# Attention beside an MLP on one core: output products in halves ahead of the values products, and a reordered VectorE queue

## The chip, the cores and the metric

One Trainium2 chip, one core of it. The metric is the time of one execution in microseconds (us) on the device. Engines: PE (TensorE: matmuls; PEld its weight loads), DVE (VectorE), ACT (ScalarE), POOL (GpSimd), SP (SyncE, which here only issues DMAs). All operands are float32; some matmuls use the float32r type, for which the kernel splits values into a high part and a low rest.

## What is computed

With x of 2048 tokens by 448 channels:

```python
g = sigmoid((x * gate_w).sum(-1, keepdims=True))
q = heads(x @ wq)            # 16 heads of 28
k = x @ wk; v = x @ wv       # one head, shared by all queries
p = softmax(q @ k.T * 28 ** -0.5)
a = (p @ v).merge_heads() @ wo
h = gelu(layernorm(x) @ w1)  # its four quarters shifted by 1, -1, 2, -2 tokens
x1 = x + shifted(h) @ w2
b = x1 + gelu(layernorm(x1) @ w3) @ w4
out = g * a + (1 - g) * b
```

## The kernel before, in words

The program has three stages on one core, and its order is the order in which the Python code issues it (manual_schedule): each engine takes its own instructions strictly in that order and waits by semaphores for the others.

1. Projections of queries, keys and values, and the shifted mixing with w1 and w2 (up to L647).
2. The MLP with w3 and w4 (L649 to L740), in four blocks of 512 tokens. The very last of its 14 column blocks isn't finished there: its gelu result is kept (gf_late, L667), and its product with w4 is done in stage 3 as a filler. At the stage's end DVE adds the accumulated products to x1 (L738).
3. Attention (L743 to the end). The 16 heads are taken in groups of four, the tokens in blocks of 512. A **unit** u is one block with one group, so there are 16 units (NU), block after block with four groups each. The 2048 keys of a unit come in 16 tiles of 128 (NT), two per pass of the loop at L862. One pass is called a **cycle** here; a unit has eight, i = 0 to 7, and c counts them from 0 to 128 over all units (the last one only finishes).

A cycle does, in this order of issue:

- score tile A (scores, L197 to L203): for four heads, three rounds of four matmuls that work beside each other on 32 rows each. Two heads land in single PSUM banks (s0, s1), two in a pair of banks (pairs[0]).
- ACT takes the exponential of s0 and of s1 (exps, L843); DVE moves the pair to SBUF (L870).
- score tile B in the same way, into s2, s3_ and pairs[1]; ACT takes the exponentials of s2, s3_, pairs[1], and last, in place, of A's moved pair.
- the values products (values, L854) of the previous cycle's two tiles, 16 matmul rows in the trace, into bank s0; DVE adds them to the unit's running sum (values_end, L784 and L786).
- extra work by i: at i = 0 the finished sums of the previous unit leave by DMA (L791); at i = 1 DVE takes their reciprocal (recip, L794) and two DMAs spread it over the partitions; at i = 3 DVE normalises the previous unit (norm, L807), and the maximum for the next unit's scores is prepared (max_part L210 and L212 in bank s1, then max_end with eight small DMAs); at i = 4 to 7 one output product each (wo_job, L817): four column-tiled matmuls of 448 columns (by_columns, L812; eight matmul rows in the trace) into s1, and one DVE instruction (L828) that weights them with the gate and adds them up; at i = 6 the queries of a later unit are split (q_begin, L194 and L195) and the next ones fetched. In unit 0 the four products of gf_late with w4 (w4_job, L834) stand in place of the output products.

The four single banks change places each cycle: what is s0, s1 in one cycle is s2, s3_ in the next (L865). So score tile B of a cycle writes the banks that the values products and the output product of the cycle before have used, and must wait until DVE has read them. The two pairs don't change.

The last unit's normalisation and output are done in a tail (from L906) that the change touches only in the names of banks and helpers.

Of the kernel before, what the change touches and what calls it, by code (L numbers as in the profile page):

```python
# [9 lines left out]
F32 = mybir.dt.float32  # L10
F32R = mybir.dt.float32r
AF = mybir.ActivationFunctionType
ALU = mybir.AluOpType
# [3 lines left out]
P = 128  # L17
# [24 lines left out]
def gated_mix_kernel(  # L42
# [206 lines left out]
    with tc.tile_pool(name="s1b", bufs=1) as s1b, \  # L249
# [263 lines left out]
        high_w2(0)  # L513
        high_w2(1)

        def first(m):
# [8 lines left out]
        stage_w1(0, first)  # L525

        def second(m):
            if m < 2:
# [120 lines left out]
    with tc.tile_pool(name="s2", bufs=1, reuse_waits="tile") as s2, \  # L649
# [36 lines left out]
        for b in range(NB):  # L686
            acc = [ps2.tile([P, 512], F32, tag="acc", bufs=4, name=f"acc_{b}_{t}") for t in range(4)]
            gs = {}
            for f in range(NF):
                if f == 9 and b + 1 < NB:  # L690
                    mv, rs = layernorm_stats(s2a, b + 1)
                if f == 10 and b + 1 < NB:
                    xt4 = big(f"xt4_{b + 1}")[:, 0:4 * D].rearrange("p (f t j) -> p f t j", f=NE, t=4)
                if f in (10, 11) and b + 1 < NB:
                    for t in (2 * f - 20, 2 * f - 19):
                        xn = s2a.tile([P, 512], F32, tag="xn", bufs=1, name=f"xn_{b + 1}_{t}")[:, 0:D]
                        layernorm_norm(b + 1, t, mv, rs, xn, xt4)
# [36 lines left out]
            for t in range(4):  # L734
                if b < NB - 1:
                    w4_part(NF - 1, t, gs[NF - 1], acc)
                xt = x1[:, 4 * b + t, :]
                nc.vector.tensor_add(xt, xt, acc[t][:, 0:D])  # L738
        assert not fills
    ctx2.close()  # L740


    with tc.tile_pool(name="s3", bufs=1, reuse_waits="tile") as s3, \  # L743
# [16 lines left out]
        def q_fetch(u):  # L760
            if u < NU:
                q_load(u, qr)
# [46 lines left out]
        def by_columns(ps, a, t, w):  # L809
            for i in range(4):  # L810
                c = t * P + 32 * i
                nc.tensor.matmul(ps[32 * i:32 * i + 32, :], a[:, c:c + 32], w, start=True, stop=True,  # L812
                                 tile_position=(0, 32 * i))

        ot_of = {}

        def wo_job(u, t, bank, end=None):  # L817
            b, g = divmod(u, NG)
            n = 4 * b + t
            ps = bank[:, 0:D]  # L820
            by_columns(ps, on_of[u], t, wof[:, g, :])
            before = x1[:, n, :] if g == 0 else ot_of[n]
            if g == 0:
                ot_of[n] = s3.tile([P, D], F32, tag="ot", bufs=5, name=f"ot_{n}")
            if end:
                end(t, n, ps, before)
                return
            nc.vector.scalar_tensor_tensor(ot_of[n], ps, gg[:, n:n + 1], before, op0=ALU.mult, op1=ALU.add)  # L828
            if g == NG - 1:
                nc.sync.dma_start(out[0, n * P:(n + 1) * P, :], ot_of[n])  # L830

        weigh_x1(NT - 4, NT)

        def w4_job(t, bank):  # L834
            n = NT - 4 + t
            ps = bank[:, 0:D]
            by_columns(ps, gf_late, t, w4_late)
            nc.vector.scalar_tensor_tensor(x1[:, n, :], ps, gi[:, n:n + 1], x1[:, n, :], op0=ALU.mult, op1=ALU.add)

        p_of = {}  # L840

# [12 lines left out]
                nc.tensor.matmul(pv[32 * j:32 * j + 32, :], vext[:, kt, :], p[:, j],  # L854
                                 start=first, stop=last, tile_position=(0, 32 * j))
# [3 lines left out]
        sums, norms = [], []  # L859
        pv = None  # L860

        for c in range(NU * NT // 2 + 1):  # L862
            u, i = divmod(c, NT // 2)
            k = 2 * c
            s0, s1, s2, s3_ = singles if c % 2 == 0 else singles[2:] + singles[:2]  # L865
            if u < NU:
                pa = score_tiles(u, 2 * i, s0, s1, pairs[0])
                exps(pa, left, s0.unsqueeze(1))
                exps(pa, right, s1.unsqueeze(1))
                nc.vector.tensor_copy(pa[:, both], pairs[0])  # L870
                pb = score_tiles(u, 2 * i + 1, s2, s3_, pairs[1])
                exps(pb, left, s2.unsqueeze(1))
                exps(pb, right, s3_.unsqueeze(1))
                exps(pb, both, pairs[1])
                exps(pa, both)
            if c:
                v = divmod(c - 1, NT // 2)[0]
                pv = s0
                values(k - 2, pv, True, False)
                values(k - 1, pv, False, True)  # L880
                if (v, i) != (NU - 1, 0):
                    values_end(v, pv)
                if i == 0 and v < NU - 1:
                    sums.append(sums_begin(v))
            if u == NU:
                break
            if i == 1 and sums:
                norms.append(recip(*sums.pop()))
            if i == 3 and norms:
                w = norms[0][0]  # L890
                norm(*norms.pop())
                jobs += [lambda bank, w=w, t=t: wo_job(w, t, bank) for t in range(4)]
            if i == 3 and u + 1 < NU:
                max_part(u + 1, range(4), s1)
                max_end(u + 1)
            elif i > 3 and jobs:
                jobs.pop(0)(s1)
            if i == 1 and u == 0:
                q_begin(1)
                q_fetch(2)  # L900
            if i == 6 and u + 2 < NU:
                q_begin(u + 2)
                q_fetch(u + 3)
        assert not sums and not norms and not jobs

        u = NU - 1  # L906
        part = o_of.pop(u)
# [4 lines left out]
        b0, b1, b2, b3 = singles  # L912
# [25 lines left out]
        def end(t, n, ps, before):  # L938
            if t == 1:
                nc.scalar.activation(y, ps, AF.Copy, scale=gg[:, n:n + 1])  # L940
                nc.gpsimd.tensor_tensor(ot_of[n], y, before, ALU.add)
            else:
                nc.vector.scalar_tensor_tensor(ot_of[n], ps, gg[:, n:n + 1], before, op0=ALU.mult, op1=ALU.add)
            queue = nc.scalar if t == 1 else nc.sync
            queue.dma_start(out[0, n * P:(n + 1) * P, :], ot_of[n])

        def tail_wo(t):
            wo_job(u, t, wo_banks[t], end)

        def keep_warm(n):  # L950
            for _ in range(n):
# [40 lines left out]
        with tc.If(again > 0, label="redo"):  # L992
            for b in range(NB):
                for g in range(NG):
# [15 lines left out]
                    banks.append(pv)  # L1010
                    norm(*recip(*sums_begin(u), False))
                    for t in range(4):
                        wo_job(u, t, bank(f"wo2_{u}_{t}"))


_OUTS = [((1, S, D), "float32")]
# [48 lines left out]
```

## Time and profile before

| | us |
|---|---|
| median of 3 runs | 963.37 (962.07 to 963.64) |
| the profiled execution | 963.59 |
| its span, first to last instruction | 961.7 |

How to read the rows: a group of instructions is given as line, engine, operation, what it writes and reads, shape and count, then busy time in us and mean ns of one, then how long the engine was idle just before them and who ended that. A row of the timeline is the start in us, the length in us, engine, line, operation, operands, count of merged instructions, and in brackets the idle time before and who ended it. Matmuls are pipelined, so their rows overlap, and a row's length is not the pace: the distance between starts is.

### The profile page before, as it was taken

How to read it: one execution, taken by the hardware profiler on the slowest of the kernel's cores; microseconds unless marked ns; L12 is line 12 of the kernel's file. 1: busy time of each engine (PE TensorE's matmuls, PEld its weight loads, DVE VectorE, ACT ScalarE, POOL GpSimd, SP SyncE). 2: the span in 40 equal slices, each digit the busy share in tenths (PEclk: the TensorE clock that was granted, in tenths of full speed). 3: DMA queues.
4: the chain of work that ended last, by engine and by line, in shares of the span. 5: the costliest groups of instructions: out<-in, count | busy, mean ns of one | idle time of the engine just before them, and what ended most of it. 6: DMA issues, size and time to landing. Idle time of an engine off the chain costs nothing.

```text
span 961.7 us, 18356 instructions
## 1 busy us (share of the span) xinstructions
PE 943.5 (98%) x7575; PEld 562.6 (59%) x7575; DVE 497.2 (52%) x766; ACT 634.2 (66%) x1005; POOL 80.9 (8%) x111
## 2 busy tenths in 40 slices
PE   9999999999999999999999999999999999999996
PEld 7788888888888888644343443344434444433432
DVE  4663454523423411265565565666566566655653
ACT  5532454322222221499989989989998998999893
POOL 3342500100003400200000000000000000000000
PEclk9999999999999999999999999999999999999999
DMA  9823452300300300100000010000010000110001
GB/s 319 274 75 92 117 175 72 102 1 1 82 2 1 82 1 1 48 12 24 14 21 14 23 50 13 23 12 23 23 52 11 14 23 12 43 32 6 9 14 42
DMA packets 40419, 46.99 MB, mean 49 GB/s; under 512 B 10120, under 2 KB 28488, under 8 KB 40328
## 3 DMA queue, kind: packets, MB, share of 16 engines
q1 hardware_dynamic: 37304, 40.27, 13.8%
q10 hardware_dynamic: 3024, 5.47, 1.6%
q8 instruction: 61, 1.00, 0.4%
q14 instruction: 30, 0.25, 0.1%
HBM read 32.56 MB, written 11.67 MB: 46 GB/s over the span
## 4 chain that ended last, share of the span: by engine, by line
PE 76%; ACT 18%; DVE 3%; issue 2%; DVEq 0%
ACT p L843 18%; PE bank L854 16%; PE bank L203 12%; PE bank L812 5%; PE acc L682 5%; PE acc L684 5%; PE acc L683 5%; PE g L135 4%; PE g L136 4%; PE g L137 4%; PE hs L460 1%; PE pair L203 1%; PE hs L461 1%; PE g L138 1%; PE g L139 1%
## 5 line engine op out<-in xcount | busy, mean ns | idle before, releaser
L843 ACT ACTIVATE p<-bank 128x512 f32<-128x512 f32 x512 | 269.9, 638 | 44.5 <-PE pair L203 37.7
L854 PE MATMUL bank<-p,vext 128*32 128x512 f32 x2048 | 247.6, 600 | 1.3
L870 DVE COPY p<-pair 128x1024 f32<-128x1024 f32 x128 | 156.0, 1219 | 18.6 <-PE pair L203 14.8
L786 DVE TENSOR_TENSOR o<-o,bank 128x512 f32<-128x512 f32 x111 | 76.3, 687 | 163.8 <-PE bank L854 162.4
L672 ACT ACTIVATE gh<-g 128x512 fp32r<-128x512 f32 x55 | 32.9, 598 | 185.0 <-PE g L139 185.0
L203 PE MATMUL bank<-qh,kh 32*128 32x512 f32 x512 | 143.9, 480 | 7.2 <-DVE mr L212 5.1
L843 ACT ACTIVATE p<-p 128x1024 f32<-128x1024 f32 x128 | 144.1, 1126 | 0.0
L203 PEld LDWEIGHTS bank<-qh,kh 32*128 32x128 f32 x512 | 61.8, 182 | 136.5 <-ACT p L843 89.1
L843 ACT ACTIVATE p<-pair 128x1024 f32<-128x1024 f32 x128 | 139.6, 1091 | 0.0
L854 PEld LDWEIGHTS bank<-p,vext 128*32 128x32 f32 x2048 | 53.8, 109 | 128.1 <-issue 77.6
L203 PE MATMUL pair<-qh,kh 32*128 32x512 f32 x512 | 128.1, 496 | 0.3 <-DVE x L738 0.3
L674 DVE TENSOR_TENSOR gl<-gf,gh 128x512 fp32r<-128x512 f32 x55 | 38.2, 695 | 166.5 <-ACT gf L673 166.5
L203 PE MATMUL bank<-ql,kh 32*128 32x512 f32 x512 | 122.5, 397 | 0.0
L203 PE MATMUL bank<-qh,kl 32*128 32x512 f32 x512 | 118.6, 390 | 0.0
L203 PE MATMUL pair<-qh,kl 32*128 32x512 f32 x512 | 101.4, 391 | 0.0
L203 PE MATMUL pair<-ql,kh 32*128 32x512 f32 x512 | 100.8, 389 | 0.0
L682 PE MATMUL acc<-w4h,gh 128*128 128x448 f32 x220 | 80.3, 365 | 0.0
L684 PE MATMUL acc<-w4h,gl 128*128 128x448 f32 x220 | 80.0, 364 | 0.0
L683 PE MATMUL acc<-w4l,gh 128*128 128x448 f32 x220 | 80.0, 363 | 0.0
L203 PEld LDWEIGHTS bank<-qh,kl 32*128 32x128 f32 x512 | 62.4, 184 | 9.3
L135 PE MATMUL g<-ah,w3h 128*128 128x512 f32 x168 | 65.8, 392 | 0.0
L136 PE MATMUL g<-al,w3h 128*128 128x512 f32 x168 | 65.7, 391 | 0.0
(199 smaller groups left out, 1398.0 us busy)
## 6 DMA issues: line engine op xcount, KB each, us to landing
qd<-qf ACTq DMA_DIRECT2D x16, 256.0 KB
rb<-rd SPq DMA_DIRECT2D x15, 256.0 KB
x<-in_x_dram SPq DMA_DIRECT2D x4, 896.0 KB
xd<-xt SPq DMA_DIRECT2D x16, 224.0 KB
w34raw<-in_w_dram SPq DMA_DIRECT2D x7, 512.0 KB
qr<-qd SPq DMA_DIRECT2D x64, 56.0 KB
out_dram<-ot SPq DMA_DIRECT2D x15, 224.0 KB
w34raw<-in_w_dram SPq DMA_DIRECT2D x7, 448.0 KB
```

The source lines that it names most:

```text
L135: nc.tensor.matmul(ps, wh[:, c, :], ah[:, c, :], start=(c == 0), stop=False)
L136: nc.tensor.matmul(ps, wh[:, c, :], al[:, c, :], start=False, stop=False)
L137: nc.tensor.matmul(ps, wl[:, c, :], ah[:, c, :], start=False, stop=False)
L203: nc.tensor.matmul(ps[j], k[h, keys], q[h, :], start=(r == 0), stop=(r == 2), tile_position=(32 * j, 0))
L682: nc.tensor.matmul(ps, gh[:, tok], w4h[i][:, k, :], start=(f == 0), stop=False)
L683: nc.tensor.matmul(ps, gh[:, tok], w4l[i][:, k, :], start=False, stop=False)
L684: nc.tensor.matmul(ps, gl[:, tok], w4h[i][:, k, :], start=False, stop=(f == stop))
L786: nc.vector.tensor_add(o_of[u], o_of[u], pv)
L812: nc.tensor.matmul(ps[32 * i:32 * i + 32, :], a[:, c:c + 32], w, start=True, stop=True, tile_position=(0, 32 * i))
L843: nc.scalar.activation(p[:, heads], p[:, heads] if source is None else source, AF.Exp, scale=SCALE)
L854: nc.tensor.matmul(pv[32 * j:32 * j + 32, :], vext[:, kt, :], p[:, j], start=first, stop=last, tile_position=(0, 32 * j))
L870: nc.vector.tensor_copy(pa[:, both], pairs[0])
```

## The change

Four edits, all in or just before stage 3:

- Output products and w4 products are cut in two column halves of 224 each: twice as many jobs of half the size. wo_job and w4_job become a part that issues the matmuls (wo_products, w4_products) and a part that issues DVE's add (wo_add, w4_add). A unit's eight halves are spread over the cycles from its i = 4 to i = 3 of the next unit, one in each, two at i = 5, none at i = 2; in the last unit two in each cycle from i = 4. Cycle 0 of unit 0, which has no values products, takes four of the eight halves of w4.
- In a cycle they stand between score tile B and the values products, in bank s0; the values products use s1. The maximum moves from i = 3 behind the values to i = 2 ahead of them (bank s0), and its end to the next cycle.
- DVE's reciprocal, normalisation, query split and end of the maximum are issued right after its move of A's pair, ahead of the half's add and of the values add.
- A four-column Exp on ACT is issued at the end of the MLP, so that the table load that comes before the first Exp stands there.

```diff
@@ end of the MLP
                 nc.vector.tensor_add(xt, xt, acc[t][:, 0:D])
+        nc.scalar.activation(first, powt, AF.Exp)
@@ jobs
-        def wo_job(u, t, bank, end=None):
+        whole = slice(0, D)
+        halves = [slice(0, D // 2), slice(D // 2, D)]
+        def wo_products(u, t, ps, cols=whole):
+            by_columns(ps[:, cols], on_of[u], t, wof[:, u % NG, cols])
+        def wo_add(u, t, ps, cols=whole, end=None):
...
-            nc.vector.scalar_tensor_tensor(ot_of[n], ps, gg[:, n:n + 1], before, op0=ALU.mult, op1=ALU.add)
+            nc.vector.scalar_tensor_tensor(ot_of[n][:, cols], ps[:, cols], gg[:, n:n + 1], before[:, cols],
+                                           op0=ALU.mult, op1=ALU.add)
...
-        jobs = [lambda bank, t=t: w4_job(t, bank) for t in range(4)]
+        jobs = [(w4_products, w4_add, (t,), cols) for t in range(4) for cols in halves]
+        MAX_AT = 2
+        TWICE = 5
+        def run_jobs(ps, n):
+            adds = []
+            for _ in range(min(n, len(jobs))):
+                products, add, args, cols = jobs.pop(0)
+                products(*args, ps, cols)
+                adds.append((add, args, cols))
+            for add, args, cols in adds:
+                add(*args, ps, cols)
@@ the loop
                 nc.vector.tensor_copy(pa[:, both], pairs[0])
+                while later:
+                    later.pop(0)()
+                if i == 1 and sums:
+                    norms.append(recip(*sums.pop()))
+                if i == 1 and u == 0:
+                    q_begin(1)
+                    q_fetch(2)
+                if i == 3 and norms:
+                    w = norms[0][0]
+                    norm(*norms.pop())
+                if i == 6 and u + 2 < NU:
+                    q_begin(u + 2)
+                    q_fetch(u + 3)
                 pb = score_tiles(u, 2 * i + 1, s2, s3_, pairs[1])
...
                 exps(pa, both)
+                if i == 4 and u:
+                    jobs += [(wo_products, wo_add, (u - 1, t), cols) for t in range(4) for cols in halves]
+                if i == MAX_AT and u + 1 < NU:
+                    max_part(u + 1, range(4), s0)
+                    later.append(lambda u=u: max_end(u + 1))
+                elif c == 0:
+                    run_jobs(s0, 2)
+                    run_jobs(s1, 2)
+                else:
+                    run_jobs(s0, 2 if i == TWICE or (u == NU - 1 and i > 3) else 1)
             if c:
...
-                pv = s0
+                pv = s1
                 values(k - 2, pv, True, False)
                 values(k - 1, pv, False, True)
...
-            if i == 1 and sums:
-                norms.append(recip(*sums.pop()))
-            if i == 3 and norms:
-                w = norms[0][0]
-                norm(*norms.pop())
-                jobs += [lambda bank, w=w, t=t: wo_job(w, t, bank) for t in range(4)]
-            if i == 3 and u + 1 < NU:
-                max_part(u + 1, range(4), s1)
-                max_end(u + 1)
-            elif i > 3 and jobs:
-                jobs.pop(0)(s1)
-            if i == 1 and u == 0:
-                q_begin(1)
-                q_fetch(2)
-            if i == 6 and u + 2 < NU:
-                q_begin(u + 2)
-                q_fetch(u + 3)
```

The rest renames: a function called first becomes first_between, since the name hid the tile first; the output tiles ot get six buffers instead of five; in the tail two bank names change places.

More of the change, by code (lines that the diff above doesn't have):

```diff
@@ L514, in gated_mix_kernel, with first_between @@
         high_w2(1)
-        def first(m):
+        def first_between(m):
             low_w2(m)
@@ L523, in first @@
                 spare_w2()
-        stage_w1(0, first)
+        stage_w1(0, first_between)
         def second(m):
@@ L815, in gated_mix_kernel, with w4_products, w4_add @@
         ot_of = {}
-        def wo_job(u, t, bank, end=None):
+        whole = slice(0, D)
[3 more added lines that the diff above has]
+        def wo_add(u, t, ps, cols=whole, end=None):
             b, g = divmod(u, NG)
             n = 4 * b + t
-            ps = bank[:, 0:D]
-            by_columns(ps, on_of[u], t, wof[:, g, :])
             before = x1[:, n, :] if g == 0 else ot_of[n]
-            if g == 0:
-                ot_of[n] = s3.tile([P, D], F32, tag="ot", bufs=5, name=f"ot_{n}")
+            if g == 0 and cols.start == 0:
+                ot_of[n] = s3.tile([P, D], F32, tag="ot", bufs=6, name=f"ot_{n}")
             if end:
-                end(t, n, ps, before)
+                end(t, n, ps[:, cols], before)
                 return
-            nc.vector.scalar_tensor_tensor(ot_of[n], ps, gg[:, n:n + 1], before, op0=ALU.mult, op1=ALU.add)
-            if g == NG - 1:
+            nc.vector.scalar_tensor_tensor(ot_of[n][:, cols], ps[:, cols], gg[:, n:n + 1], before[:, cols],
+                                           op0=ALU.mult, op1=ALU.add)
+            if g == NG - 1 and cols.stop == D:
                 nc.sync.dma_start(out[0, n * P:(n + 1) * P, :], ot_of[n])
         weigh_x1(NT - 4, NT)
-        def w4_job(t, bank):
+        def w4_products(t, ps, cols):
+            by_columns(ps[:, cols], gf_late, t, w4_late[:, cols])
+        def w4_add(t, ps, cols):
             n = NT - 4 + t
-            ps = bank[:, 0:D]
-            by_columns(ps, gf_late, t, w4_late)
-            nc.vector.scalar_tensor_tensor(x1[:, n, :], ps, gi[:, n:n + 1], x1[:, n, :], op0=ALU.mult, op1=ALU.add)
+            nc.vector.scalar_tensor_tensor(x1[:, n, cols], ps[:, cols], gi[:, n:n + 1], x1[:, n, cols],
+                                           op0=ALU.mult, op1=ALU.add)
         p_of = {}
@@ L886, in gated_mix_kernel @@
                 break
[L887 to L904 removed]
+        assert not sums and not norms and not jobs and not later
         u = NU - 1
@@ L947, in tail_wo @@
         def tail_wo(t):
-            wo_job(u, t, wo_banks[t], end)
+            wo_products(u, t, wo_banks[t])
+            wo_add(u, t, wo_banks[t], end=end)
         def keep_warm(n):
@@ L1012, in gated_mix_kernel @@
                     for t in range(4):
-                        wo_job(u, t, bank(f"wo2_{u}_{t}"))
+                        ps = bank(f"wo2_{u}_{t}")
+                        wo_products(u, t, ps)
+                        wo_add(u, t, ps)
 _OUTS = [((1, S, D), "float32")]
```

6 lines of the change are left out of this document (3 added, 3 removed).

## The prediction

> **What bounds the kernel now.** I read the page first: the share of each engine, then the chain that ended last, then the costliest groups.
>
> ```profile
> span 961.7 us, 18356 instructions
> PE 943.5 (98%) x7575; PEld 562.6 (59%) x7575; DVE 497.2 (52%) x766; ACT 634.2 (66%) x1005; POOL 80.9 (8%) x111
> PE 76%; ACT 18%; DVE 3%; issue 2%; DVEq 0%
> L843 ACT ACTIVATE p<-bank 128x512 f32<-128x512 f32 x512 | 269.9, 638 | 44.5 <-PE pair L203 37.7
> ```
>
> PE carries three quarters of the chain and ACT the rest; the ACT group says where they change places: it idles 44.5 us ahead of its exponentials, nearly all of it waiting for PE. So there are cycles (passes of the loop at L862) that PE sets and cycles that ACT sets. To price them I read the timeline of one whole unit (eight cycles). First the starts of the values products L854, once per cycle:
>
> ```profile
> 481.99 1.92 PE L854 MATMUL bank<-p,vext 128*32 128x512 f32 x16
> 486.87 1.92 PE L854 MATMUL bank<-p,vext 128*32 128x512 f32 x16
> 491.33 1.92 PE L854 MATMUL bank<-p,vext 128*32 128x512 f32 x16
> 495.79 1.92 PE L854 MATMUL bank<-p,vext 128*32 128x512 f32 x16
> ...
> 504.69 1.92 PE L854 MATMUL bank<-p,vext 128*32 128x512 f32 x16
> 508.37 1.92 PE L854 MATMUL bank<-p,vext 128*32 128x512 f32 x16
> ...
> 515.99 1.92 PE L854 MATMUL bank<-p,vext 128*32 128x512 f32 x16
> ```
>
> A unit is 515.99 - 481.99 = 34.00 us. The step that holds the maximum takes 4.88, one that holds a whole output product 4.46 (491.33 to 495.79), one without 3.68. Inside a cycle without a product:
>
> ```profile
> 502.85 0.50 PE L203 MATMUL bank<-qh,kh 32*128 32x512 f32 x2
> ...
> 503.80 0.50 PE L203 MATMUL pair<-qh,kh 32*128 32x512 f32 x2
> ...
> 503.90 2.06 ACT L843 ACTIVATE p<-bank 128x512 f32<-128x512 f32 x4 [0.53 <-PE pair L203]
> ...
> 506.54 0.50 PE L203 MATMUL bank<-qh,kh 32*128 32x512 f32 x2
> ...
> 506.74 0.69 DVE L786 TENSOR_TENSOR o<-o,bank 128x512 f32<-128x512 f32 x1 [1.59 <-PE bank L854]
> ...
> 507.48 0.50 PE L203 MATMUL bank<-qh,kh 32*128 32x512 f32 x2
> ...
> 507.68 2.10 ACT L843 ACTIVATE p<-bank 128x512 f32<-128x512 f32 x4
> 511.44 1.17 ACT L843 ACTIVATE p<-bank 128x512 f32<-128x512 f32 x2
> ```
>
> Call a cycle's two score tiles A and B, and count from A's start (502.85). ACT begins A's exponentials at +1.05, the values products start at +1.84 (504.69), the next A at +3.69 (506.54). B of that next cycle starts only 0.94 after its A (507.48), because its bank is freed by DVE's values add (506.74 + 0.69 = 507.43). So PE, with this DVE step inside its loop, needs **3.69** a cycle; ACT needs 511.44 - 507.68 = **3.76**. They are almost equal, and every microsecond of PE work put into single cycles shows in full.
>
> **The change, part by part.**
>
> *Products in halves.* Before, four cycles of a unit carry a whole product and the other four none.
>
> ```profile
> 493.07 0.94 PE L812 MATMUL bank<-wof,on 128*32 128x448 f32 x8
> 493.08 0.13 PEld L812 LDWEIGHTS bank<-wof,on 128*32 128x32 f32 x4 [0.30 <-issue]
> ```
>
> A whole product costs 4.46 - 3.69 = 0.77. A half has the same eight matmuls and loads, with 224 columns instead of 448. Bounds: 0.77 if the columns don't matter, 0.38 if they alone do. I take **0.38**, the row being a steady stream: the four loads of the second group take 0.13 from 493.08, under the first group's matmuls, and half a group still lasts 0.19. Sum of halves in a unit: 8 x 0.38, as much PE work as before; what is won is that it no longer stands in four cycles, where ACT waits for PE, while PE waits for ACT in others (3.76 instead of 3.69).
>
> *Order inside a cycle.* The half now stands between B and the values, in the first bank, and the values in the second. The half waits for ACT's first exponential and the values for its second. Four exponentials take 2.06 in all, one 0.64 (the mean in the ACT group above), so they start 0.47 apart and the second ends at +1.05 + 0.47 + 0.64 = +2.16. The half ends at +1.84 + 0.38 = +2.22, so the new wait is just covered; in a cycle without a half it isn't, and the values start at about +2.20. Cycle lengths by this, with 1.85 from values to the next A:
> - one half: 3.69 + 0.38 = 4.07; two halves: 4.45
> - none: 2.20 + 1.85 = 4.05 (0.29 more than ACT's 3.76 now)
>
> DVE gets two half adds for each whole one:
>
> ```profile
> L828 DVE SCALAR_TENSOR_TENSOR ot<-bank,gg,ot 128x448 f32<-128x448 f32 x44 | 30.1, 683 | 3.4
> L955 DVE TENSOR_TENSOR oo<-o,bank 128x128 f32<-128x128 f32 x4 | 0.9, 282 | 1.7 <-PE bank L854 1.7
> L807 DVE TENSOR_TENSOR on<-o,rb 128x512 f32<-128x512 f32 x15 | 10.3, 685 | 0.0
> L870 DVE COPY p<-pair 128x1024 f32<-128x1024 f32 x128 | 156.0, 1219 | 18.6 <-PE pair L203 14.8
> ```
>
> A half add lies between 0.28 (128 columns) and 0.68 (448); by the line through both, 0.40 is my estimate. It runs beside the values products (1.85), so it costs nothing as long as the values add behind it isn't late.
>
> *The maximum.* Its four matmuls move from the second bank, behind the values, to the first, ahead of them.
>
> ```profile
> 483.84 0.66 PE L210 MATMUL bank<-khd,qh 128*128 128x128 f32 x4
> 484.43 0.50 PE L203 MATMUL bank<-qh,kh 32*128 32x512 f32 x2
> 485.24 0.68 DVE L212 TENSOR_REDUCE mr<-bank 128x16 f32<-128x512 f32 x1
> 485.98 0.50 PE L203 MATMUL bank<-qh,kh 32*128 32x512 f32 x1 [0.36 <-DVE mr L212]
> ```
>
> On PE they cost 484.43 - 483.84 = 0.59. Today B then stands until 485.98, 1.55 after its A instead of 0.94, for DVE's reduce, which is queued behind the values add and the normalisation. Afterwards the reduce runs during the values, and that 0.61 goes: 3.69 + 0.59 = 4.28 instead of 4.88.
>
> ```profile
> L240 DVE STREAM_TRANSPOSE mrow<-mc 128x32 f32<-128x32 f32 x16 | 3.4, 212 | 0.6
> L798 DVE RECIPROCAL rr<-rt 128x16 f32<-128x16 f32 x15 | 3.7, 246 | 0.0
> ```
>
> *DVE's other work* (reciprocal, normalisation, the end of the maximum, the split of queries) goes ahead of the half add and the values add, behind the move of scores. That move ends at about +1.07 + 1.22 = +2.29; the values add is wanted at +4.07 + 0.20 = +4.27. In the fullest cycle (i = 3) between them stand the end of the maximum (three small instructions of which the longest takes 0.21, so about 0.6), the normalisation 0.69 and a half add 0.40: +3.98. Covered by 0.3. The reciprocal now follows its DMA more closely:
>
> ```profile
> 507.45 0.58 SPq L791 DMA_DIRECT2D rt<-o  x1
> 511.40 0.34 SPq L800 DMA_DIRECT2D rd<-rr  x1
> 512.82 0.55 SPq L802 DMA_DIRECT2D rb<-rd  x1
> ```
>
> The sums leave at 507.45, in the next cycle's terms +0.9. An 8 KB transfer like it (L800) was down 1.42 later, when L802 could go; so it is there at about +2.4, when DVE gets to it. Check and reciprocal take 0.4 (L798 has 0.25), the half add 0.4: +3.2, covered. SP issues the same transfers in the same order, the broadcast earlier than before, so the normalisation two cycles on has it.
>
> *The start.*
>
> ```profile
> 400.53 1.28 ACT L843 ACT_TABLE_LOAD   x1 [5.75 <-PE bank L203]
> ...
> 403.45 0.98 PE L203 MATMUL bank<-qh,kh 32*128 32x512 f32 x2 [2.07 <-ACT p L843]
> 404.00:408.00 4.00, 4.00 (x35) 0.57 0.03 8
> ...
> 408.94 0.50 PE L203 MATMUL bank<-qh,kh 32*128 32x512 f32 x2
> ```
>
> The load stands on the path: ACT was idle for 5.75 before it. At the end of the MLP it lies in that idle time and costs nothing. PE's 2.07 of idling, after which its clock shows 0.57 for four microseconds (third row, its last figures are clock, DMA share and GB/s), is filled by four halves, 4 x 0.38 from about 401.3 to 402.8. Then cycle 1 starts at 402.9, ACT is free at 400.53 + 3.76 = 404.29, its second exponential is done at 404.29 + 0.47 + 0.64 = 405.4, and the third A starts at about 405.45 + 1.85 = 407.3 instead of 408.94: **-1.6**.
>
> *Sum.* The last cycle's A stands at
>
> ```profile
> 939.64 0.50 PE L203 MATMUL bank<-qh,kh 32*128 32x512 f32 x2
> ```
>
> so the 125 cycles between took 939.64 - 408.94 = 530.70. The same afterwards: rest of unit 0: 4.28 + 3 x 4.07 + 2 x 4.05 = 24.6; unit 1 (products from its fifth cycle): 3 x 4.05 + 4.28 + 3 x 4.07 + 4.45 = 33.1; units 2 to 14: 6 x 4.07 + 4.45 + 4.28 = 33.15 each (0.85 less than now), 431.0; unit 15, which does its own predecessor's halves in pairs: 3 x 4.07 + 4.05 + 3 x 4.45 = 29.6. Together 518.3, **-12.4**. From the last A to the end nothing is changed in length: the last exponentials set it. With the start -14.0. The profiled execution took 963.59 (1.9 outside its span), 0.2 over the median of 963.37: 963.59 - 14.0 = **949.6**.
>
> **Rivals.**
>
> *DVE comes late.* Cover is 0.3 at i = 3, about 1 at i = 1. If a transfer lands later or the half add is nearer 0.68, the values add is late and B with it, which PE then pays. 0.4 us a unit gives 955.6, 0.7 gives 960. For it: DVE is the third engine in PE's loop, and its queue is in order. Against: only three of eight cycles carry such work.
>
> *Slower: a half doesn't cost half.* Place: the eight matmuls of each half; if the weight loads of a group (0.13) are not hidden under the shorter one ahead, a half costs 0.38 + 2 x 0.13 = 0.64, cycles 4.33 and 4.97, a unit 35.2, and the time 981. With 121 halves in the 125 cycles it decides from 14.0 / 121 = 0.12 more, so a half at 0.50. Against it stands the L812 load row above: loads begin with the group ahead, and a whole group keeps its pace.
> [...]
>
> *It doesn't do what it says.* If the products can't stand ahead of the values without the values waiting as long (the second exponential later than +2.16 by 0.15), all 125 cycles grow by 0.1 and 12.4 goes: the start alone remains, 962.
>
> *More.* If B no longer waited for the values add (0.15 a cycle), 125 x 0.15 = 19 more: 931. Against: that add still follows the values.
>
> **How the numbers follow.** Forecast, 946 to 953: 0.62. DVE late, up to 960: 0.22. Half not half: 0.08. Start alone: 0.05. More: 0.03. The unknown costs move the forecast by 125 x 0.03 = 4 either way, so the range runs from 945 to 960 and leaves out 0.16. A measurement tells about 0.2% (1.9 us) from no change: faster 0.87, same 0.05, slower 0.08.
>
> **What would show it.** Right: values starts 4.07 apart in six cycles of a unit, 4.28 and 4.45 in the two others, units of 33.15; PE waiting for DVE's reduce no more; the table load ahead of 397 and the clock at 1.00 from 404 to 408; a half's two groups 0.19 apart. Wrong: half matmul groups 0.25 apart or more; B more than 0.95 behind A in cycles i = 1, 3, 6; the values waiting for ACT by more than 0.05 in cycles with a half; a check or normalisation that waits for a DMA.

## The result and the profile after

The changed kernel takes **949.14 us** (median of 4 runs, 948.92 to 949.26) against 963.43 of the kernel before (962.07 to 963.64): a ratio of 0.9854, 95% interval 0.9837 to 0.9871. The forecast was 949.6. The profiled execution took 949.08. Each ratio below is to executions of the kernel before made beside that run (medians 963.29 to 963.73), without two slow ones of 1491 and 3135 us.

From the page of the kernel after, the span, the chain that ended last, and the group of ACT's exponentials:

```profile
span 947.3 us, 19530 instructions
...
PE 97%; ACT 1%; DVE 0%; DMA 0%; issue 0%; DVEq 0%
...
L850 ACT ACTIVATE p<-bank 128x512 f32<-128x512 f32 x512 | 264.6, 603 | 33.0 <-PE pair L203 14.6
```

The chain now lies on PE for 97% instead of 76%: the cycles that ACT set are gone. Ahead of these exponentials ACT waits 14.6 us for PE's pair of score tiles, where it waited 37.7. Now the start of stage 3, from the timeline of the kernel after:

```profile
395.15 1.28 ACT L739 ACT_TABLE_LOAD   x1
...
400.90 2.06 ACT L850 ACTIVATE p<-bank 128x512 f32<-128x512 f32 x4 [4.25 <-POOL good L774]
401.66 1.72 PE L813 MATMUL bank<-w_late,gf_late 128*32 128x224 f32 x32
403.31 0.50 PE L203 MATMUL bank<-qh,kh 32*128 32x512 f32 x2
...
407.70 0.51 PE L203 MATMUL bank<-qh,kh 32*128 32x512 f32 x2
```

The table load stands at 395.15, in ACT's idle time; the four halves of w4 (32 matmul rows) fill PE from 401.66 to 403.31; the third A starts at 407.70. And the row of the stretch that showed a clock of 0.57 before:

```profile
404.00:408.00 4.00, 4.00 (x48) 1.43 (x44) 3.15 (x6) 4.00 (x7) 1.54 (x2) 1.00 0.07 15
```

The clock (third figure from the end) stays at 1.00, and PE has 48 rows in it instead of 35. In the middle of the stage, a cycle with the maximum and one with a half:

```profile
540.17 0.50 PE L203 MATMUL bank<-qh,kh 32*128 32x512 f32 x2
...
541.12 0.50 PE L203 MATMUL pair<-qh,kh 32*128 32x512 f32 x2
...
542.02 0.66 PE L210 MATMUL bank<-khd,qh 128*128 128x128 f32 x4
542.61 1.92 PE L861 MATMUL bank<-p,vext 128*32 128x512 f32 x16
542.79 0.69 DVE L212 TENSOR_REDUCE mr<-bank 128x16 f32<-128x512 f32 x1 [0.33 <-ACT p L850]
...
544.47 0.50 PE L203 MATMUL bank<-qh,kh 32*128 32x512 f32 x2
...
544.66 0.69 DVE L787 TENSOR_TENSOR o<-o,bank 128x512 f32<-128x512 f32 x1 [1.18 <-PE bank L861]
...
545.41 0.50 PE L203 MATMUL pair<-qh,kh 32*128 32x512 f32 x2
...
546.29 0.59 PE L813 MATMUL bank<-wof,on 128*32 128x224 f32 x8
...
546.70 1.90 PE L861 MATMUL bank<-p,vext 128*32 128x512 f32 x16
...
547.79 0.44 DVE L832 SCALAR_TENSOR_TENSOR ot<-bank,gg,ot 128x224 f32<-128x224 f32 x1
...
548.53 0.50 PE L203 MATMUL bank<-qh,kh 32*128 32x512 f32 x2
```

The cycle with the maximum runs from 540.17 to 544.47 (4.30), the one with a half from 544.47 to 548.53 (4.06). DVE's reduce now lies beside the values products, and B stands 0.94 behind its A (545.41 to 544.47), as it did in a plain cycle before. It is still held by DVE: the values add ends at 544.66 + 0.69 = 545.35. (Here and below B is counted from its matmuls into the bank that DVE reads last; the matmul into the other bank, free earlier, starts already at 545.27.)

For the comparison of runs, the time from the first A of stage 3 to the third ("start"), from there to the last A ("125 cycles"), and the length of a unit in its middle, all read from the starts of L203 in the timeline of each kernel's profiled execution (e8 ran once):

| kernel | median us | start | 125 cycles | unit |
|---|---|---|---|---|
| before | 963.43 | 10.01 | 530.70 | 34.00 |
| after | 949.14 | 8.41 | 518.96 | 33.15 |
| e1, whole products | 965.07 | 8.68 | 534.17 | 34.20 |
| e2, quarters | 953.01 | 8.74 | 520.26 | 33.20 |
| e3, halves behind | 949.06 | 8.31 | 518.42 | 33.19 |
| e4, maximum behind | 954.77 | 8.42 | 524.28 | 33.53 |
| e5, Exp late | 951.11 | 9.70 | 519.38 | 33.16 |
| e6, before with Exp early | 960.93 | 7.93 | 530.62 | 34.00 |
| e7, DVE's work behind | 950.12 | 8.41 | 518.94 | 33.15 |
| e8, banks swapped | 990.5 | 8.79 | 559.24 | 36.02 |
| e9, before with DVE's order | 955.04 | 9.92 | 523.47 | 33.38 |
| e10, before with halves | 963.66 | 10.53 | 529.69 | 33.95 |
| e11, values split | 944.74 | 9.40 | 512.26 | 32.86 |
| e12, e11 with DVE's work behind | 938.25 | 8.32 | 506.55 | 32.43 |

In e11's start, 1.0 us goes to a single wait in unit 0: DVE's query split (L194) waits for the DMA of the queries, ahead of the first values add.

### The profile page after: what moved, and what is told of

It reads as the page before. It is cut to its first block, busy times and chain, and to the rows that moved or that the text cites. A ratio compares the mean times of both kernels' runs of the same rounds, so it can differ in the third digit from the quotient of the medians.

```text
span 947.3 us, 19530 instructions
## 1 busy us (share of the span) xinstructions
PE 936.6 (99%) x8087; PEld 580.0 (61%) x8087; DVE 509.9 (54%) x830; ACT 638.3 (67%) x1006; POOL 80.8 (9%) x111
## 4 chain that ended last, share of the span: by engine, by line
PE 97%; ACT 1%; DVE 0%; DMA 0%; issue 0%; DVEq 0%
PE bank L861 24%; PE bank L203 21%; PE bank L813 7%; PE acc L682 5%; PE acc L684 5%; PE acc L683 5%; PE g L135 4%; PE g L136 4%; PE g L137 4%; PE pair L203 3%; PE hs L460 1%; PE hs L461 1%; PE g L138 1%; PE g L139 1%; PE h L135 1%; PE h L136 1%
## 5 line engine op out<-in xcount | busy, mean ns | idle before, releaser
L850 ACT ACTIVATE p<-bank 128x512 f32<-128x512 f32 x512 | 264.6, 603 | 33.0 <-PE pair L203 14.6
L861 PE MATMUL bank<-p,vext 128*32 128x512 f32 x2048 | 244.2, 593 | 1.7 <-ACT p L850 1.7
L203 PEld LDWEIGHTS bank<-qh,kh 32*128 32x128 f32 x512 | 70.1, 182 | 135.2 <-ACT p L850 106.0
L203 PE MATMUL bank<-qh,kh 32*128 32x512 f32 x512 | 146.4, 469 | 0.2
L850 ACT ACTIVATE p<-p 128x1024 f32<-128x1024 f32 x128 | 139.6, 1091 | 0.0
L850 ACT ACTIVATE p<-pair 128x1024 f32<-128x1024 f32 x128 | 135.1, 1055 | 0.0
L203 PE MATMUL bank<-ql,kh 32*128 32x512 f32 x512 | 132.1, 395 | 0.0
L203 PE MATMUL pair<-qh,kh 32*128 32x512 f32 x512 | 128.0, 495 | 0.3 <-DVE x L738 0.3
L203 PE MATMUL bank<-qh,kl 32*128 32x512 f32 x512 | 128.2, 388 | 0.0
L861 PEld LDWEIGHTS bank<-p,vext 128*32 128x32 f32 x2048 | 57.9, 109 | 102.5 <-issue 77.1
L203 PE MATMUL pair<-qh,kl 32*128 32x512 f32 x512 | 101.2, 390 | 0.0
L203 PE MATMUL pair<-ql,kh 32*128 32x512 f32 x512 | 100.5, 387 | 0.0
L203 PEld LDWEIGHTS bank<-qh,kl 32*128 32x128 f32 x512 | 70.6, 183 | 7.9
L813 PE MATMUL bank<-wof,on 128*32 128x224 f32 (+1 forms) x992 | 70.2, 369 | 0.0
```

The lines of the kernel that those rows point to most:

```text
L203: nc.tensor.matmul(ps[j], k[h, keys], q[h, :], start=(r == 0), stop=(r == 2), tile_position=(32 * j, 0))
L850: nc.scalar.activation(p[:, heads], p[:, heads] if source is None else source, AF.Exp, scale=SCALE)
```

## The experiments

**e1, whole products ahead of the values.** Are halves needed at all?

```diff
-        halves = [slice(0, D // 2), slice(D // 2, D)]
+        halves = [whole]
...
-                    run_jobs(s0, 2 if i == TWICE or (u == NU - 1 and i > 3) else 1)
+                    run_jobs(s0, 1)
```

> Whole output products (448 columns) instead of halves, one in each of the cycles i = 4 to 7 as before the change, but ahead of the values products as after it. Theory (PE's loop sets every cycle, and a product costs its columns wherever it stands, so spreading halves is what pays): four cycles of 3.69 + 0.77 = 4.46, three without a product at 4.05 because the values wait for the second exponential, the maximum's at 4.28: a unit of 34.3 instead of 33.15, time about 965, no better than before. Rival (the gain is in the order ahead of the values and in the maximum, not in the halving): 949 to 951.

965.07 us (963.81 to 966.07; ratio to before 1.0018 [1.0008, 1.0027]), as expected. In the timeline of e1, a cycle without a product:

```profile
547.71 0.50 PE L203 MATMUL bank<-qh,kh 32*128 32x512 f32 x2
...
549.91 1.92 PE L861 MATMUL bank<-p,vext 128*32 128x512 f32 x16 [0.29 <-ACT p L850]
...
551.76 0.50 PE L203 MATMUL bank<-qh,kh 32*128 32x512 f32 x2
```

The values wait 0.29 for ACT's second exponential, and the cycle takes 4.05 with no product in it. Three such cycles, the maximum's of 4.30 and four of 4.44 with a product make a unit of 34.2: the four edits with whole products lose time. (No run has whole products behind the values with the maximum ahead of them.) The wait behind the bank is what the half fills.

**e2, quarters, two to a cycle.** Does cutting have a price of its own?

```diff
-        halves = [slice(0, D // 2), slice(D // 2, D)]
+        halves = [slice(k * D // 4, (k + 1) * D // 4) for k in range(4)]
...
-                    run_jobs(s0, 2 if i == TWICE or (u == NU - 1 and i > 3) else 1)
+                    run_jobs(s0, 4 if i == TWICE or (u == NU - 1 and i > 3) else 2)
```

> Quarters (112 columns), two in each cycle where after has one half, four where it has two. Theory (columns alone are paid): the same 949 within 1. Rival (weight loads are not hidden below the 0.13 that four of them take): a quarter's group streams 0.09, so each of the 32 groups of a unit loses about 0.04, 1.2 us a unit, about 967.

953.01 us (950.35 to 953.42; ratio 0.9881 [0.9862, 0.9901]). The time missed my expectation of 949 within 1. But the unit is 33.20 against 33.15: 0.05 more for twice as many loads and matmuls, so the rival is out. That is 0.8 of the 3.9 us over 15 units. In the profiled execution the largest part, 2.2, lies ahead of stage 3 (its first A at 401.47 instead of 399.29), where the two kernels are alike; it is told under the hardware below.

**e3, halves behind the values.** What is the place ahead of the values worth?

```diff
-                else:
-                    run_jobs(s0, 2 if i == TWICE or (u == NU - 1 and i > 3) else 1)
...
-                pv = s1
+                pv = s1 if u < NU and maxed else s0
...
+            if c and not maxed:
+                run_jobs(s1, 2 if i == TWICE or (u == NU - 1 and i > 3) else 1)
```

> The halves go back behind the values products (values in the first bank, half in the second); the maximum stays ahead of the values, DVE's other work stays ahead. Theory (B is held by DVE's values add, 0.94 behind its A): a half behind the values lets PE work while DVE adds; B then waits for the half's add, 0.86 behind its A, and the values wait for the first exponential alone: 3.99 a cycle instead of 4.07, a unit of 32.65, about 942. Rival (a product behind the values makes B wait for its add as before the change, so the place ahead of the values is part of the gain): 949 or more, up to 955.

949.06 us (948.82 to 949.66; ratio 0.9847 [0.983, 0.9863]): no difference from after, and my theory, 942, fell. The timeline of e3 shows why:

```profile
547.84 0.69 DVE L787 TENSOR_TENSOR o<-o,bank 128x512 f32<-128x512 f32 x1 [0.49 <-PE bank L861]
548.00 0.50 PE L203 MATMUL bank<-qh,kh 32*128 32x512 f32 x2
...
548.44 0.45 DVE L832 SCALAR_TENSOR_TENSOR ot<-bank,gg,ot 128x224 f32<-128x224 f32 x1
...
548.95 0.50 PE L203 MATMUL pair<-qh,kh 32*128 32x512 f32 x2
```

The values add now is early, but the half's add comes last: it ends at 548.44 + 0.45 = 548.89, and B stands at 548.95, again 0.95 behind its A. B waits for DVE's last read of the two banks, whichever instruction that is.

**e4, the maximum behind the values again** (at i = 3, its end still in the next cycle; the half of i = 3 goes to i = 2).

```diff
-                if i == MAX_AT and u + 1 < NU:
-                    max_part(u + 1, range(4), s0)
...
+            if i == 3 and u + 1 < NU:
+                max_part(u + 1, range(4), s0)
+                later.append(lambda u=u: max_end(u + 1))
```

> After, but the maximum's matmuls and reduce stand behind the values again, at i = 3 (first bank), and the half of i = 3 moves to i = 2. Theory (before the change B was held 0.61 because the normalisation stood between the values add and the reduce; with the normalisation ahead only about 0.1 of it returns, and the values of that cycle wait for the second exponential): the maximum's cycle 4.65 to 4.7 instead of 4.28, about 955. Rival (the stall belongs to a reduce behind the values as such): 0.6 more on top, about 963.

954.77 us (953.99 to 955.43; ratio 0.9904 [0.9888, 0.9921]), as expected: 5.6 us of after's gain hang on the place of the maximum. The unit grows by 0.38 to 33.53. From the timeline of e4:

```profile
547.64 1.92 PE L861 MATMUL bank<-p,vext 128*32 128x512 f32 x16 [0.29 <-ACT p L850]
...
550.09 0.50 PE L203 MATMUL bank<-qh,kh 32*128 32x512 f32 x2
...
551.04 0.50 PE L203 MATMUL pair<-qh,kh 32*128 32x512 f32 x2
```

B doesn't wait longer for DVE's reduce: it stands 0.95 behind its A, thanks to DVE's order. What is lost is the filling: with nothing ahead of them, the values of this cycle wait 0.29 for the second exponential, as in e1.

**e5, the table load late** (after without the first Exp) and **e6, the table load early** (before with it):

```diff
         nc.vector.tensor_add(xt, xt, acc[t][:, 0:D])
+        nc.scalar.activation(first, powt, AF.Exp)
```

> After without the early Exp: the table load stands on the path again. Theory: the first exponential comes 1.28 later, the four halves of cycle 0 wait for it, PE idles about 1.2 instead of the 2.07 of before and keeps its clock: 950.4. Rival (this idling also brings the slow clock for some 3.4 us): 951.5 to 952.5.

> The kernel before with the early Exp alone. Theory: 1.28 less for ACT, PE's 2.07 of idling shrinks to about 1.2 and its clock stays up, so the third A comes 2.1 earlier: 961.3 (before 963.4). Rival (the load alone, the clock still falls): 962.1.

e5 took 951.11 us (950.52 to 952.25; ratio 0.9871 [0.9856, 0.9886]), e6 960.93 (960.35 to 962.13; ratio 0.9979 [0.9969, 0.9988]). The starts are 9.70 instead of 8.41, and 7.93 instead of 10.01. PE's idle time there, from the timeline of e5 and of e6:

```profile
402.97 1.72 PE L812 MATMUL bank<-w_late,gf_late 128*32 128x224 f32 x32 [1.10 <-ACT p L849]
```

```profile
402.33 0.98 PE L203 MATMUL bank<-qh,kh 32*128 32x512 f32 x2 [0.81 <-ACT p L844]
```

e5's median lies between the theory and the rival, but its start grew by 1.29, as the theory had it; e6 came out by the theory. Both keep a clock of 1.00, where before's 2.07 of idling was followed by 3.41 us at half. So e6 alone has 2.08 at the start; after has 1.60, with its four halves of w4 in that stretch (1.72 in the row at 401.66).

**e7, DVE's other work behind the values add again** (with the maximum ahead).

```diff
-                while later:
-                    later.pop(0)()
-                if i == 1 and sums:
-                    norms.append(recip(*sums.pop()))
...
+            while later:
+                later.pop(0)()
+            if i == 1 and sums:
+                norms.append(recip(*sums.pop()))
```

> After, but DVE's reciprocal, normalisation, query split and end of the maximum stand behind the values add again. Theory (DVE has cover either way: the move of scores then starts 0.5 to 1.0 later in three cycles of a unit and still ends before ACT needs it): 949.1 within 1. Rival (the reorder is part of the gain, each of three cycles of a unit longer by 0.3 to 0.5): 963 to 971.

950.12 us (949.25 to 952.64; ratio 0.9871 [0.9855, 0.9887]); 125 cycles in 518.94 against 518.96 (the first A came 0.5 later), so the stage is as the theory had it. With the maximum ahead of the values, DVE's order no longer matters.

**e8, the two banks swapped** (half and maximum in s1, values in s0).

```diff
-                    run_jobs(s0, 2 if i == TWICE or (u == NU - 1 and i > 3) else 1)
+                    run_jobs(s1, 2 if i == TWICE or (u == NU - 1 and i > 3) else 1)
...
-                pv = s1
+                pv = s0
```

> After with the two banks exchanged: half and maximum in the second bank, values in the first. Theory (PE stands just behind ACT's second exponential): half and maximum start 0.36 later in their cycles, a unit of about 36, about 985 to 990. Rival (the exponentials are done in time, only PE and DVE count): 949 to 951.

990.5 us in a single run: the unit is 36.02, a cycle with a half 4.42. From the timeline of e8:

```profile
569.12 0.59 PE L813 MATMUL bank<-wof,on 128*32 128x224 f32 x8 [0.35 <-ACT p L850]
...
569.52 1.90 PE L861 MATMUL bank<-p,vext 128*32 128x512 f32 x16
```

The half waits 0.35 for the second exponential, and the values behind it have the wait in full. The half has to stand in the bank that ACT empties first.

**e9, only DVE's order** (before, with DVE's other work and the end of the maximum moved as in after) and **e10, only the halves** (before, with halves behind the values, spread as in after).

```diff
                 nc.vector.tensor_copy(pa[:, both], pairs[0])
+                while later:
+                    later.pop(0)()
+                if i == 1 and sums:
+                    norms.append(recip(*sums.pop()))
...
-                max_end(u + 1)
+                later.append(lambda u=u: max_end(u + 1))
```

```diff
-            elif i > 3 and jobs:
-                jobs.pop(0)(s1)
+            elif c:
+                run_jobs(s1, 2 if i == TWICE or (u == NU - 1 and i > 3) else 1)
```

> The kernel before (whole products behind the values, maximum behind them at i = 3, late table load) with only DVE's reciprocal, normalisation, query split and end of the maximum moved behind the move of scores. Theory (0.61 of the old 4.88 cycle is the normalisation standing between the values add and the reduce): B is held about 0.1 instead of 0.61 in one cycle of a unit, 33.5 instead of 34.0, about 955.5. Rival (this order is worth nothing by itself, as putting it back behind the values in the changed kernel cost nothing, and halving and place bring the gain): 961 to 963.5.

> The kernel before with halves instead of whole products, behind the values, spread over all cycles but i = 3; maximum, DVE's order and table load as before. Theory (halving wins only what ACT-bound cycles lose now, 0.07 to 0.12 in each of three cycles of a unit): 33.7 a unit, about 959. Rival (spreading the products is most of the change's gain of 14): 951 to 953.

e9 took 955.04 us (954.23 to 956.98; ratio 0.9916 [0.9899, 0.9932]), as expected; e10 took 963.66 (962.24 to 966.01; ratio 1.001 [0.9999, 1.002]), and missed both its theory and its rival. The cycle after the maximum, from the timeline of e9 and then of e10:

```profile
550.25 0.50 PE L203 MATMUL bank<-qh,kh 32*128 32x512 f32 x2
...
550.45 0.69 DVE L212 TENSOR_REDUCE mr<-bank 128x16 f32<-128x512 f32 x1
...
551.20 0.50 PE L203 MATMUL pair<-qh,kh 32*128 32x512 f32 x2
```

```profile
485.23 0.50 PE L203 MATMUL bank<-qh,kh 32*128 32x512 f32 x2
...
485.44 0.69 DVE L807 TENSOR_TENSOR on<-o,rb 128x512 f32<-128x512 f32 x1
...
486.04 0.69 DVE L212 TENSOR_REDUCE mr<-bank 128x16 f32<-128x512 f32 x1
...
486.78 0.49 PE L203 MATMUL bank<-qh,kh 32*128 32x512 f32 x1 [0.36 <-DVE mr L212]
486.79 0.50 PE L203 MATMUL pair<-qh,kh 32*128 32x512 f32 x2
```

In e9 the reduce directly follows the values add and B stands 0.95 behind its A; in e10 the normalisation is still ahead of it and B stands 1.56 behind. That is the 0.61 a unit. In e10 the halves shorten some cycles and DVE takes it back in others: from i = 0 they last 4.06, 4.04, 4.22, 4.26, 4.68, 4.44, 4.20, 4.05. A cycle with a half that DVE doesn't delay takes 4.05; i = 3 holds the maximum and i = 5 two halves, so the delays stand at i = 2, 4 and 6.

**e11, the values products split by tokens.** Since B waits for DVE's last read (e3), the values are put into both banks, 256 tokens each, so that the first half of the add runs under the second half of the products, and the output half goes behind them into s0:

```diff
-                values(k - 2, pv, True, False)
-                values(k - 1, pv, False, True)
-                if (v, i) != (NU - 1, 0):
-                    values_end(v, pv)
+                pv = [s0, s1]
+                for ps, cols in zip(pv, tokens):
+                    values_half(k - 2, ps, cols, True, False)
+                    values_half(k - 1, ps, cols, False, True)
+                    if (v, i) != (NU - 1, 0):
+                        values_add(v, ps, cols)
...
+            elif c:
+                run_jobs(s0, 2 if i == TWICE or (u == NU - 1 and i > 3) else 1)
```

> A new arrangement on top of the change: the values products are made for 256 tokens at a time, the first half into the first bank and the second into the second, so that DVE adds the first while PE makes the second; half products and the maximum stand behind them in the first bank. Theory (B's 0.95 behind its A is DVE's add after PE's last work, 0.16 more than the 0.79 that A itself takes; with only half an add left after the values that goes): a cycle with a half 3.95 instead of 4.07, a unit of about 32.2 instead of 33.15, about 935. Rival (PE's own switch between tile shapes sets the 0.95, or twice the matmuls and loads cost more than is won): 949 or more.

944.74 us (943.84 to 946.42; ratio 0.9808 [0.9794, 0.9821]): faster than after, but not by what I expected. Cycles with one half fell to 3.95, as worked out, with two exceptions in each unit, i = 3 (4.31) and i = 6 (4.26). The cycle i = 3 in the timeline of e11:

```profile
547.04 0.65 DVE L808 TENSOR_TENSOR on<-o,rb 128x512 f32<-128x512 f32 x1
...
547.61 0.92 DVE L882 TENSOR_TENSOR o<-o,bank 128x256 f32<-128x256 f32 x2
548.08 0.59 PE L813 MATMUL bank<-wof,on 128*32 128x224 f32 x8
...
548.59 0.50 PE L203 MATMUL bank<-qh,kh 32*128 32x512 f32 x2
...
549.40 0.39 PE L203 MATMUL pair<-qh,kh 32*128 32x512 f32 x2
```

B stands 0.81 behind its A (0.95 in after). But the normalisation holds up the first half of the values add, and the output half, which uses the same bank, waits for it.

**e12, e11 with DVE's other work behind again.**

```diff
-                if i == 3 and norms:
-                    w = norms[0][0]
-                    norm(*norms.pop())
...
+            if i == 3 and norms:
+                w = norms[0][0]
+                norm(*norms.pop())
```

> e11 with DVE's reciprocal, normalisation, query split and end of the maximum put back behind the half's add, as in e7. Theory (in e11 these delay the first half of the values add in the cycles i = 3, 4.32 us, and i = 6, 4.26 us, and the product in the same bank waits for that add; behind the half's add they have cover): those cycles fall to about 3.95, a unit of about 32.2 us instead of 32.9, and the kernel takes 932 to 936 us (2 us either way for the start of the clock). Rival (their order doesn't matter, or the moves of scores come late instead): 943 to 945 us or more.

**938.25 us** (936.81 to 939.52; ratio to before 0.9739 [0.9722, 0.9757]): the fastest of all. The cycle i = 3 fell to 4.00, but i = 6 only to 4.14, and the unit to 32.43 instead of 32.2; 14 units of 0.23 are 3.2 of the 4.3 us by which it stands above the middle of what I expected. The cycle behind the two halves, in the timeline of e12:

```profile
552.64 0.50 PE L203 MATMUL bank<-qh,kh 32*128 32x512 f32 x2
...
552.78 0.81 DVE L832 SCALAR_TENSOR_TENSOR ot<-bank,gg,ot 128x224 f32<-128x224 f32 x2 [0.28 <-PE bank L813]
...
553.64 0.19 PEld L203 LDWEIGHTS bank<-qh,kh 32*128 32x128 f32 x2 [0.47 <-DVE ot L832]
553.64 0.50 PE L203 MATMUL bank<-qh,kh 32*128 32x512 f32 x2
```

Two half adds end at 553.59, and B follows at 553.64, 1.00 behind its A. So 0.2 of the stall of i = 6 belongs to the two half adds of the cycle before; moving the query split took only 0.12 off it (4.26 to 4.14). Of the 6.5 us from e11 to e12, about 1 is, by the profiled executions, e11's wait for the queries in unit 0. What would remove the rest of the stall (two halves in two banks, or another spread) wasn't tried.

## Why the prediction was right

The profiled executions differ by 961.7 - 947.3 = 14.4 us: the way to the first A +0.36, the start -1.60, the 125 cycles -11.74, the rest to the end -1.44. Forecast were 0, -1.6, -12.4 and 0. Point by point:

- *Half costs half, 0.38:* right. Cycles with a half take 4.06 to 4.08 (forecast 4.07), with two 4.44 to 4.45 (4.45). As a cycle without a half would take 4.05, the price of a half shows only in the second one: 4.45 - 4.07 = 0.38. Starts of L203 in the kernel after, of the cycle with two (i = 5) and of the next:

```profile
585.75 0.50 PE L203 MATMUL bank<-qh,kh 32*128 32x512 f32 x2
...
590.20 0.50 PE L203 MATMUL bank<-qh,kh 32*128 32x512 f32 x2
```

  Quarters (e2) bear it out: loads and matmuls doubled again cost 0.05 a unit. The rival that pays for the loads had a unit of 35.2 with halves; it is 33.15, as forecast without such a cost, and 33.20 with quarters. In the timeline of after, a half's eight loads take 0.16 from 546.29, beside its matmuls of 546.29 to 546.88. What hides the loads, the runs don't show.
- *Cycles without a half, 4.05:* right, shown by e1's cycles of 4.05 with 0.29 of waiting for the second exponential.
- *B stays 0.94 behind its A:* right for a reason that I hadn't thought through. I took the values add to be what holds it; e3 shows that it is the last read of DVE in either bank, so that the place ahead of the values gains nothing by itself. It is one of two equal orders (949.14 and 949.06).
- *The maximum, 4.28, and 0.61 a unit:* right in size (4.29 to 4.30). But the edit has two ways to the same end, and I gave the credit to one: e9 gets the 0.61 with the maximum still behind the values, by the order of DVE's queue; e7 gets it with the old order, by the place of the maximum. What the place does beyond that is fill the wait ahead of the values, 0.38 a unit (e4).
- *DVE's cover, the largest rival:* it held. The half add takes 0.44 to 0.45 (L832 in after and e3) and not 0.40; at i = 3 the end of the maximum, the normalisation and the half add are done at 547.79 + 0.44 = 548.23, 0.51 ahead of the values add at 548.74, where I had 0.3. One of my signs of failure did show, the check waiting for its DMA, from the waits of the kernel after:

```profile
DVE good L778 <- DMA rt<-o: 8.0, 15, 0.8
```

  15 waits of up to 0.8 us; they fit into the cover of about 1 that i = 1 has, and its cycle stays at 4.07.
- *The start, -1.6:* right, 10.01 to 8.41.
- *The sum:* 0.7 of the 12.4 is missing, because two of the 125 cycles took 4.79 and 4.42 instead of 4.44 and 4.07. In the first, the values add starts 0.54 behind A instead of 0.2 and B with it; its row names the products as what it waited for, and theirs show no delay. Fourteen cycles that are 0.34 to 0.37 too long stand in the profiles of after, e1 to e5, e7 and e10. In each of them a transfer of 8 KB on the instruction queue q14 starts 0.8 to 1.7 behind A (in after at 520.54 and 603.62). But 13 of after's 15 transfers of this kind in units 1 to 14 delay nothing, so the cause stays open. A single cycle of 5.50 in e9 is another case: there the normalisation waited 2.15 for its DMA, a transfer that the prediction took to be down in time.
- *The last 1.44* were not forecast, and belong to no edit: the time from the last A to the end was 20.4 to 22.1 in these runs without order, and what differs is how long the issue of the last output transfer takes (below).

Where the gain came from: about 2 us from the table load and the clock (e6), about 8 from the maximum's stall (e9). The halves by themselves bring nothing (e10), and in whole products the same order loses (e1). What was left, 33.38 to 33.15 a unit, came with the halves and the maximum's place together: halves with the new order, but the maximum behind the values, have 33.53 (e4), more than whole products in that order (e9). That this rest comes from filling every cycle alike, so that ACT no longer waits in one and PE in the next, fits the cycle lengths, but no run tests it by itself.

## What to carry to other kernels

In a loop where three engines hand two banks around, look for the last reader of a bank. Here moving another reader changed nothing (e3), and ending the last read earlier, with DVE's other work out of its way, gave 10.9 us more than the four edits (e12). Spreading work evenly over the cycles paid here only once the stall of single cycles was gone (e10), so remove the stall first, and price each edit alone as well as together. A filler that stands in a wait was free only up to the wait's length (a second half costs 0.38), and only in the bank that comes free first (e8).

## What the runs showed of the hardware

**A slow start of varying length.** The first products of stage 1 ran at half pace for a time that differs from run to run, and the first A of stage 3 comes at times up to 2.82 us apart. The stretch from 6 to 8 us, in the kernel after and in e2:

```profile
6.00:8.00 2.00, 2.00 (x6) 0.95 (x5) 1.29 (x2) 1.14 (x2) 0.00 (x0) 1.00 1.01 343
```

```profile
6.00:8.00 2.00, 2.00 (x3) 0.67 (x2) 1.08 (x2) 1.42 (x3) 0.00 (x0) 1.00 1.03 388
```

PE is busy throughout in both, with six matmul rows and with three, though the column of the clock has 1.00 in both. The column counts time without a record of the clock as 1.00, and the first record, of the full clock, begins at 4.53 in after and at 9.19 in e2. The first A of stage 3 came at 401.47 in e2 and 401.38 in e11, whose records begin latest (9.19 and 9.10), and at 398.65 to 399.79 in the others (3.79 to 6.43). Single executions can't tell 2 us here; the starts inside a stage can.

**The fall of the clock.** The clock fell to half for 3.41 us in the three profiles in which PE had idled 2.07 or 2.08 us at the start of stage 3 (before, e9, e10) and in none with 0.81 or 1.10 (e6, e5). The fall doesn't come at once: in before PE worked again from 403.45, and the clock fell at 404.40. In before the fall and the return (407.81) stand 117 and 118 times 3.413 us behind the first record (5.04), and the change near the end (957.36) 279 times; the only change in after (943.20) stands 275 times that behind its first record. In the 3.41 us that ended with the fall PE was busy for 1.35 in before and 1.33 in e9; in the 3.41 us around e5's 1.10 of idling (401.64 to 405.05), without a fall, for 2.31. Of idle times between 1.10 and 2.07 these five profiles show nothing.

**The last transfers.** SyncE issues the last output transfer 14.3 to 14.8 us behind the last A in all runs. The instruction that issues it took 0.33 in the kernel after and 1.93 in e12, and in before 1.86:

```profile
941.04 0.33 SPq L969 DMA_DIRECT2D out_dram<-ot  x1
```

```profile
928.68 1.93 SPq L992 DMA_DIRECT2D out_dram<-ot  x1
```

It took 0.33 in four of the 14 profiles (after, e2, e7, e11), whose time from the last A to the end is 20.4 to 20.6, and 1.19 to 1.93 in the ten others, with 21.3 to 22.1. So before's 1.86 against 0.33 holds the 1.44 that the forecast didn't have. Why the length differs isn't shown.
